# Order of TensorE's work in a two-layer gated network: output matmuls in one run of 24

## The chip, the cores and the metric

The kernel runs on one core of a Trainium2 chip. The metric is the time of one execution in device microseconds (us); of several runs the median is given. Names of engines are those of the profile: PE is TensorE (matmuls), ACT is ScalarE, DVE is VectorE, POOL is GpSimd, SP is the queue from which the transfers are issued.

## What is computed

An attention with a feature map feeds two gated networks, one after the other. Cut to what matters:

```python
def _attn_ref(q, k, v, w_phi):          # 4 batches, 8 heads, 576 tokens, 64 per head
    def phi(x):
        proj = np.einsum('bhsd,df->bhsf', x, w_phi)
        proj = proj - np.max(np.abs(proj), axis=-1, keepdims=True)
        return np.concatenate([np.exp(proj), np.exp(-proj)], axis=-1)
    q_p, k_p = (phi(q), phi(k))
    kv = np.einsum('bhsf,bhsd->bhfd', k_p, v)
    z = np.sum(k_p, axis=2)
    num = np.einsum('bhsf,bhfd->bhsd', q_p, kv)
    den = np.einsum('bhsf,bhf->bhs', q_p, z)[..., None] + 1e-06
    return (num / den).astype(np.float32)

def _moe_ref(x, w_gate, w_val, w_out):  # x: 2304 x 512; w: 512 x 1536; w_out: 1536 x 512
    g = x @ w_gate
    silu = g * (1.0 / (1.0 + np.exp(-g)))
    return (silu * (x @ w_val)) @ w_out
# _moe2_ref: the same with the gate 1 / (1 + exp(-g))
```

## The kernel before

**Two stages.** The attention takes the first 150 us or so, and the two networks the rest. While the attention runs, the weights of the first network are brought in, and its last matmuls (`ratio`) mix with the first products of the network.

**Units.** The network stage is a list of 60 units. There are four passes `hh` (two networks, each with two halves of the 1536 inner columns), five token blocks `j` in each (four of 512 tokens, called wide, and one of 256), and three slots `p` of 256 inner columns for each block. So 48 units are wide and 12 are not.

**What a wide unit does.** Its gate and value projections are not plain matrix products: both operands are cut into 2 x 2 quarters and multiplied with seven products in place of eight. The products are numbered 1 to 7. Each is 12 matmuls of 256 columns (`product`, line 1031): two halves `w` (gate and value), two depths `c`, and three matmuls for a float32 product, since every operand is held as a high and a low part (`xh`, `xl`, `w0h`, `w0l`). Products 1, 6, 7 and 4 add up in one PSUM bank `a`; 5 and 3 in a bank `b`; 2 in another bank `b`. Between them, what stands in a bank is taken out:

- `keep` (line 1051, ACT) copies a bank to SBUF tiles `c0`, `c1` after products 1, 5 and 6. After product 1 it must be done before product 6 goes on in the same bank, after 5 before 3, and after 6 before 7.
- `add` (line 1057, DVE) adds a bank to what was kept, after products 2, 3 and 7.
- `gate` (line 1069, ACT), `gated` (line 1074, DVE), and then `high` (line 583, a cast on ACT) and `rest` (line 577, a subtraction on DVE) make the high and low parts `uh0`, `ul0` (after product 2) and `uh1`, `ul1` (after product 4) of the hidden layer. Each of `c0`, `c1`, `uh0`, `ul0`, `uh1`, `ul1` is one buffer that all units share.

**Output matmuls.** The hidden layer of a unit goes through the output weights (`accumulate`, lines 1107 and 1109) while the next unit's products run: four groups "a", "b" (from `uh0`, `ul0`), "c", "d" (from `uh1`, `ul1`), six matmuls of 512 columns each in a wide unit. They add up in four PSUM banks, two tiles `c` and two `d`, over the three slots of a block, and are copied out after the third. The matmul form prints the same letters a to d for tiles; groups are in quotes here.

**What sets the order.** `ORDER` gives the order of products and groups within a unit: its first row is for the narrow units, its second for the wide ones. In a wide unit the 24 output matmuls of the unit before come in three runs: "a" and "b" (12) after products 1 and 5; "c" and half of "d" (9) after products 6, 3, 7, 2; the other half (3) after product 4. The last unit has an order of its own, `ORDER_LAST`. All instructions of the kernel, of every engine and of the transfers, are then issued in the order of a table of numbers, `TIMES`: one number for each call, sorted. The engines take their instructions in that order and wait for each other by semaphores.

Of the kernel before, what the change touches and what calls it, by code (L numbers as in the profile page):

```python
# [77 lines left out]
         (1, 5, "a", "b", 6, 3, 7, 2, "c", "d0", 4, "d1"))  # L78
# [7 lines left out]
def as_float(bits):  # L86
# [19 lines left out]
        118, 162, 249, 206, 954, 788, 1147, 1464, 2497, 1852, 2540, 3132, 3460, 3878, 3977, 4525,  # L106
        4833, 5378, 5684, 6173, 6591, 7102, 7522, 7945, 8102, 8691, 9544, 9068, 9633, 10226,
        10554, 11015, 11321, 11889, 12425, 12860,),
    "load_v": (
        292, 380, 1748, 2142, 2822, 3644, 4633, 5487, 6418, 6998, 7418, 8360, 9332, 10334, 11124,  # L110
        11785, 12191, 13289,),
    "proj": (
        601, 768, 1038, 1278, 1743, 2388, 2176, 3023, 3338, 3737, 3868, 4416, 4722, 5270, 5575,
        6065, 6482, 6993, 7413, 7837, 7925, 8582, 8933, 9436, 9524, 10117, 10416, 10907, 11212,
        11780, 12311, 12751, 13072, 13473, 14052, 14573,),
    "shift": (
        788, 1027, 1300, 1573, 2078, 2497, 2736, 3171, 3471, 3922, 4161, 4598, 4985, 5402, 5802,
        6276, 6667, 7220, 7526, 8027, 8266, 8691, 9108, 9555, 9795, 10287, 10606, 11019, 11436,
        12002, 12420, 12860, 13180, 13670, 14161, 14882,),
    "exps": (  # L120
        1038, 1189, 1283, 1433, 1748, 1856, 2329, 2450, 3053, 3239, 3732, 3882, 4664, 4814, 5487,
        5637, 6400, 6521, 7027, 7147, 7875, 8001, 8555, 8829, 9450, 9571, 10376, 10497, 11152,
        11273, 11785, 11935, 12700, 12987, 13431, 13552,),
    "k_sum": (
# [3 lines left out]
    "kv_keep": (  # L128
        2423, 2544, 3854, 4032, 5825, 5853, 7549, 7576, 9544, 9665, 11246, 11367, 13081, 13109,
        15224, 15252,),  # L130
    "turn": (
        1832, 2817, 3427, 4328, 5181, 5976, 6694, 7502, 8355, 9022, 10028, 10818, 11869, 12663,
        13561, 13963, 14484, 15219,),
    "turn_exp": (
# [4 lines left out]
    "ratio": (  # L139
# [4 lines left out]
    "ratio_out": (  # L144
# [4 lines left out]
    "ratio_store": (  # L149
# [4 lines left out]
    "den_load": (  # L154
        4790, 7042, 8889, 10598, 12468, 14658, 15446, 17825,),
    "den_inv": (
        5258, 8539, 10188, 11292, 13099, 15499, 16090, 18567,),
    "den_store": (
        5308, 8589, 10269, 11364, 13149, 15549, 16339, 18617,),
    "part_banks": (  # L160
        15433, 14716,),
    "swap": (
        15219, 17295,),
    "product": (
# [259 lines left out]
    "load_num": (  # L424
        13536, 13715, 16100, 16427, 19004, 21522, 23433, 24018, 27139, 29781,),
    "norm": (
        14400, 14460, 14761, 14821, 17132, 16837, 17192, 17620, 19596, 19562, 22152, 22186, 24214,
        24275, 24789, 24850, 27844, 27905, 30547, 30487,),
    "keep_x": (
        14532, 14897, 17235, 17692, 19641, 22318, 25949, 26375, 30041, 30467,),  # L430
# [885 lines left out]
```

## Time and profile before

| | us |
|---|---|
| median of 3 runs | 988.04 (987.86 to 988.91) |
| the profiled execution | 988.43 |
| its span, from the first to the last instruction | 986.5 |
| PE busy in it | 971.2 (98%) |
| DVE, ACT, POOL busy | 692.1 (70%), 527.6 (53%), 38.8 (4%) |
| transfers' share of 16 engines | 42.9% |
| granted TensorE clock | 1.00 of full speed |

Nearly all of the span PE is busy, in matmuls that are given to it in a fixed order. Busy time of pipelined matmuls overlaps: a matmul's row lasts 0.28 or 0.39 us, but the next one starts 0.11 or 0.23 us after it. So it is the distance between starts that tells what PE does. The rows below come from the timeline (one row for an instruction), from the chain of work that ended last (merged, with the time each piece adds), and from views that group.

### The profile page before, as it was taken

How to read it: one execution, taken by the hardware profiler on the slowest of the kernel's cores; microseconds unless marked ns; L12 is line 12 of the kernel's file. 1: busy time of each engine (PE TensorE's matmuls, PEld its weight loads, DVE VectorE, ACT ScalarE, POOL GpSimd, SP SyncE). 2: the span in 40 equal slices, each digit the busy share in tenths (PEclk: the TensorE clock that was granted, in tenths of full speed). 3: DMA queues.
4: the chain of work that ended last, by engine and by line, in shares of the span. 5: the costliest groups of instructions: out<-in, count | busy, mean ns of one | idle time of the engine just before them, and what ended most of it. 6: DMA issues, size and time to landing. Idle time of an engine off the chain costs nothing.

```text
span 986.5 us, 20911 instructions
## 1 busy us (share of the span) xinstructions
PE 971.2 (98%) x8632; PEld 883.4 (90%) x8632; DVE 692.1 (70%) x1220; ACT 527.6 (53%) x977; POOL 38.8 (4%) x40
## 2 busy tenths in 40 slices
PE   6999999999999999999999999999999999999998
PEld 6777778999999999999999999999999999999997
DVE  6989889838758795368787996576768734555343
ACT  5988878535545564354554664554546434324322
POOL 1433210000000000000000000000000000000000
PEclk9999999999999999999999999999999999999999
DMA  7566876436535532066554451546316103132011
GB/s 243 167 216 210 257 231 219 151 126 173 207 118 158 186 98 81 12 208 218 153 176 145 159 166 51 161 145 209 117 65 192 44 1 99 52 129 86 1 44 43
DMA packets 67551, 136.00 MB, mean 138 GB/s; under 512 B 9408, under 2 KB 35712, under 8 KB 67456
## 3 DMA queue, kind: packets, MB, share of 16 engines
q1 hardware_dynamic: 67456, 134.68, 42.9%
q8 instruction: 67, 1.10, 0.5%
q14 instruction: 28, 0.23, 0.1%
HBM read 94.66 MB, written 39.99 MB: 136 GB/s over the span
## 4 chain that ended last, share of the span: by engine, by line
PE 92%; DVE 6%; DMA 1%; issue 1%; ACT 0%; SPq 0%; DVEq 0%; ACTq 0%
PE a L1031 30%; PE b L1031 23%; PE c L1109 8%; PE c L1107 7%; PE d L1107 7%; PE d L1109 6%; PE d L794 4%; PE w L695 3%; PE c L731 3%; DVE sub L704 2%; DVE m L702 2%; PE w L758 1%; DMA raw<-wpk 1%; DVE w1l L577 0%; DMA x<-kT 0%
## 5 line engine op out<-in xcount | busy, mean ns | idle before, releaser
L1057 DVE TENSOR_TENSOR c<-b,c 128x512 f32<-128x512 f32 x96 | 66.0, 687 | 115.6 <-PE b L1031 108.7
L1069 ACT ACTIVATE c<-c 128x256 f32<-128x256 f32 x96 | 50.4, 526 | 145.2 <-DVE c L1057 145.2
L1051 ACT COPY c<-a 128x512 f32<-128x512 f32 x96 | 56.5, 588 | 109.1 <-PE a L1031 107.1
L577 DVE TENSOR_TENSOR ul<-c,uh 128x512 fp32r<-128x512 f32 (+1 forms) x120 | 75.8, 635 | 32.1 <-ACT uh L583 31.3
L583 ACT CAST uh<-c 128x512 fp32r<-128x512 f32 (+1 forms) x120 | 69.3, 580 | 41.7 <-DVE c L1074 32.2
L1031 PE MATMUL a<-xh,w0h 128*128 128x256 f32 x288 | 80.5, 279 | 0.0
L1031 PE MATMUL a<-xh,w1h 128*128 128x256 f32 x288 | 80.4, 279 | 0.0
L1031 PE MATMUL a<-xh,w2h 128*128 128x256 f32 x288 | 80.3, 279 | 0.0
L1031 PE MATMUL a<-xl,w0h 128*128 128x256 f32 x288 | 80.0, 278 | 0.0
L1031 PE MATMUL a<-xl,w1h 128*128 128x256 f32 x288 | 80.0, 278 | 0.0
L1031 PE MATMUL a<-xl,w2h 128*128 128x256 f32 x288 | 80.0, 278 | 0.0
L1031 PE MATMUL a<-xh,w0l 128*128 128x256 f32 x288 | 79.9, 277 | 0.0
L1031 PE MATMUL a<-xh,w1l 128*128 128x256 f32 x288 | 79.9, 277 | 0.0
L1031 PE MATMUL a<-xh,w2l 128*128 128x256 f32 x288 | 79.8, 277 | 0.0
L1074 DVE TENSOR_TENSOR c<-c 128x256 f32<-128x256 f32 (+1 forms) x96 | 53.0, 555 | 29.5 <-ACT c L1069 29.4
L1031 PE MATMUL b<-xh,w0h 128*128 128x256 f32 x224 | 62.1, 277 | 0.0
L1031 PE MATMUL b<-xh,w0l 128*128 128x256 f32 x224 | 62.0, 277 | 0.0
L1031 PE MATMUL b<-xl,w0h 128*128 128x256 f32 x224 | 62.0, 277 | 0.0
L1031 PE MATMUL b<-xh,w1l 128*128 128x256 f32 x224 | 61.9, 276 | 0.0
L1031 PE MATMUL b<-xh,w2l 128*128 128x256 f32 x224 | 61.9, 276 | 0.0
L1031 PE MATMUL b<-xh,w1h 128*128 128x256 f32 x224 | 61.9, 276 | 0.0
L1031 PE MATMUL b<-xl,w1h 128*128 128x256 f32 x224 | 61.9, 276 | 0.0
(183 smaller groups left out, 3019.7 us busy)
## 6 DMA issues: line engine op xcount, KB each, us to landing
raw<-wpk SPq DMA_DIRECT2D x72, 512.0 KB, 4.9
wf<-wcv SPq DMA_DIRECT2D x40, 256.0 KB, 2.8
a<-wf SPq DMA_DIRECT2D x20, 512.0 KB, 5.4
b<-xo SPq DMA_DIRECT2D x16, 512.0 KB, 6.9
part<-o SPq DMA_DIRECT2D x13, 512.0 KB, 6.3
o<-part SPq DMA_DIRECT2D x13, 512.0 KB, 5.3
wfo<-wcv SPq DMA_DIRECT2D x20, 256.0 KB, 5.0
v<-v SPq DMA_DIRECT2D x18, 264.0 KB, 6.6
```

The costliest lines, as they stand in the source:

```text
L577: nc.vector.tensor_tensor(out=lo, in0=src, in1=hi, op=ALU.subtract)
L583: nc.scalar.copy(hi, src)
L695: nc.tensor.matmul(r["ps"][:, i, n, c], r["x"][d, c, n * P:(n + 1) * P], w2[d], start=True, stop=True)
L731: nc.tensor.matmul(kv[qd, b][h // 2][u * 64:(u + 1) * 64, c * P:c * P + VW], e[r0:r1, h % 2, n, h // 2, s, u], r["v"][r0:r1, n, h], start= ...
L794: nc.tensor.matmul(pn[i * w:(i + 1) * w, :m], f, e[:, h, c, :m], start=(c == 0), stop=(c == 1))
L1031: nc.tensor.matmul(o, f[:, c], x[:, c], start=k == first and w == 0 and c == 0 and m == 0, stop=c == 1 and m == 2, skip_group_check=True)
L1051: nc.scalar.copy(part_of(r, d), parts(r, src))
L1057: nc.vector.tensor_tensor(out=c, in0=parts(r, "zy x"[d]), in1=c, op=ALU.add)
L1069: nc.scalar.activation(o, g, AF.Silu if hh < 2 else AF.Sigmoid)
L1074: nc.vector.tensor_tensor(out=o, in0=v, in1=places(r, j, 0, d)[1], op=ALU.mult)
L1107: nc.tensor.matmul(ps[:, :n], a[:, k], x, start=st, stop=sp)
L1109: nc.tensor.matmul(ps, x[:, k], a, start=st, stop=sp)
```

## The change

The wide row of `ORDER` is rewritten. Products 1, 5, 6, 3, 7, 2 now follow each other, all 24 output matmuls of the unit before come then in one run, and product 4 closes the unit. The order inside "a" to "d" and in a product is the same, and no matmul, copy or transfer is added or taken away. Narrow units and the last unit keep their rows. The table `TIMES` is new throughout, also for the attention; two of its rows are shown.

```diff
 ORDER = ((1, 2, "a", "b", 5, "c", "d", 4),
-         (1, 5, "a", "b", 6, 3, 7, 2, "c", "d0", 4, "d1"))
+         (1, 5, 6, 3, 7, 2, "a", "b", "c", "d", 4))
 ORDER_LAST = (1, 5, "a", 6, 3, "b", 7, 2, "c", 4, "d")
...
     "keep": (
-        15525, 15863, 16115, 16969, 17030, 17681, 18686, 18790, 19190, 20150, 20287, 20699, 21669,
...
+        15453, 15579, 15784, 16705, 16765, 17612, 18573, 18710, 18884, 20082, 20219, 20356, 21591,
```

**PE, the second unit of the fourth block in the first pass.** Each row is the first of a product's 12 matmuls, of 6 in a group, or of 3 of one bank; `a` and `b` are product banks, `c` and `d` output banks, numbers tell buffers apart. Before:

```order
L1031 MATMUL a_4146<-xh_3627,w1h0_1242 128x256
L1031 MATMUL b_4167<-xh_3627,w1h0_1242 128x256 [waits PE_49]
L1107 MATMUL c_4183<-uh0_4142,o0h0_968 128x512 [waits Activation_49]
...
L1031 MATMUL a_4146<-xh_3627,w1h0_1242 128x256 [waits Activation_49]
L1031 MATMUL b_4167<-xh_3627,w1h0_1242 128x256 [waits Activation_49]
...
L1031 MATMUL b_4241<-xh_3627,w1h0_1242 128x256 [waits PE_49]
L1107 MATMUL c_4183<-uh1_4163,o0h0_968 128x512
...
L1031 MATMUL a_4146<-xh_3627,w1h0_1242 128x256 [waits DVE_49]
L1107 MATMUL d_4197<-uh1_4163,o0h0_968 128x512
L1031 MATMUL a_4312<-xh_3627,w2h0_2645 128x256
```

and now:

```order
L1028 MATMUL a_4140<-xh_3629,w1h0_1238 128x256
L1028 MATMUL b_4158<-xh_3629,w1h0_1238 128x256 [waits PE_49]
L1028 MATMUL a_4140<-xh_3629,w1h0_1238 128x256 [waits Activation_49]
L1028 MATMUL b_4158<-xh_3629,w1h0_1238 128x256 [waits Activation_49]
...
L1028 MATMUL b_4218<-xh_3629,w1h0_1238 128x256 [waits DVE_49]
L1104 MATMUL c_4239<-uh0_4109,o0h0_945 128x512
L1104 MATMUL c_4239<-ul0_4110,o0h0_945 128x512 [waits DVE_49]
...
L1104 MATMUL c_4239<-uh1_4154,o0h0_945 128x512
...
L1028 MATMUL a_4140<-xh_3629,w1h0_1238 128x256 [waits DVE_49]
L1028 MATMUL a_4303<-xh_3629,w2h0_2665 128x256
```

The output matmuls have left the place between products 5 and 6 and the place behind product 4. Products 6 and 3, which wait for ACT's copies, stand now one product behind the product that those copies empty, as product 7 did already. In the whole program a product follows a 512-column matmul at 151 places before and at 64 now.

**ACT, the third unit of the fourth block in the third pass (the copies of the unit, `L1051` before and `L1048` now, and what stands around them).** `uh` casts make the hidden layer's high part, `xh` casts that of the next block's x, `wcv` and `raw` are steps of the weights' preparation. Before:

```order
L1069 ACTIVATE c1_8777<-a_8726 128x256 [waits PE_49]
L583 CAST uh1_8919<-c1_8777 128x512 [waits DVE_49,PE_49]
L1051 COPY c0_8930<-a_8904 128x2x256 [waits PE_49,Activation_49]
L583 CAST xh_8812<-b_8867 128x256 [waits DMAHW4_49]
L583 CAST xh_8812<-b_8867 128x512
L532 ACTIVATE wcv_8951<-raw_8747 128x512 [waits DMAHW6_49]
L1051 COPY c1_8953<-b_8922 128x2x256 [waits DVE_49,PE_49]
```

and now:

```order
L1066 ACTIVATE c1_8775<-a_8735 128x256 [waits PE_49]
L580 CAST xh_8808<-b_8852 128x256 [waits DMAHW4_49]
L580 CAST xh_8808<-b_8852 128x512
L580 CAST xh_8808<-b_8852 128x256 [waits DVE_49]
L1048 COPY c0_8935<-a_8910 128x2x256 [waits PE_49,Activation_49]
L580 CAST uh1_8944<-c1_8775 128x512 [waits DVE_49]
L580 CAST xh_8808<-t_8902 128x512
L580 CAST xh_8808<-t_8902 128x256
L1048 COPY c1_8966<-b_8926 128x2x256 [waits DVE_49,PE_49]
L1048 COPY c0_8935<-a_8910 128x2x256 [waits PE_49]
```

Here five casts of x stand between the gate and the copy after product 5, where two casts and a step of the weights stood. Over all wide units but the first, ACT has 79 such other instructions between the last gate and the copy after product 5 in 28 units before, and 41 in 19 units now; in the others the row is gate, `uh1` cast, copy, copy, copy.

## Rows read from the trace of the kernel before

**Rows 1.** Windows: length; busy us and instructions of PE, PEld, DVE, ACT, POOL; clock, DMA.

```profile
128.00:172.00 44.00, 44.00 (x597) 33.69 (x594) 39.18 (x68) 35.51 (x71) 1.53 (x2) 1.00 0.75 226
172.00:983.00 811.00, 810.55 (x5858) 759.42 (x5856) 538.77 (x1020) 388.59 (x735) 0.00 (x0) 1.00 0.37 120
```

**Rows 2.** Waits of PE from 172 to 983 us: total, times, longest.

```profile
PE c L1107 <- DVE ul L577: 0.2, 1, 0.2
```

**Rows 3.** Chain that ended last, one wide unit: start, us added, engine, matmuls.

```profile
295.93 1.39 PE a L1031 x12
...
298.00 1.39 PE a L1031 x12
299.39 1.36 PE b L1031 x12
300.75 1.37 PE c L1107 x6
302.12 1.37 PE d L1107 x6
303.50 1.39 PE a L1031 x12
304.88 1.36 PE b L1031 x12
...
311.02 1.39 PE a L1031 x12
```

**Rows 4.** PE timeline around two waits for the low part: start, us, matmul.

```profile
249.17 0.39 PE L1107 MATMUL c<-uh,o2h 128*128 128x512 f32 x1
249.50 0.50 PE L1107 MATMUL c<-ul,o2h 128*128 128x512 f32 x1
249.84 0.39 PE L1107 MATMUL c<-uh,o2l 128*128 128x512 f32 x1
...
360.96 0.39 PE L1107 MATMUL c<-uh,o2h 128*128 128x512 f32 x1
361.55 0.50 PE L1107 MATMUL c<-ul,o2h 128*128 128x512 f32 x1 [0.20 <-DVE ul L577]
361.89 0.39 PE L1107 MATMUL c<-uh,o2l 128*128 128x512 f32 x1
```

**Rows 5.** Timeline of one undisturbed wide unit, last matmuls of products 4 and 1 (PE).

```profile
739.97 0.28 PE L1031 MATMUL a<-xh,w0l 128*128 128x256 f32 x1
...
742.04 0.28 PE L1031 MATMUL a<-xh,w1l 128*128 128x256 f32 x1
```

**Rows 6.** The same on ACT: gate, cast, copies after products 1 and 5.

```profile
740.28 0.39 ACT L1069 ACTIVATE c<-a 128x256 f32<-128x256 f32 x1 [0.45 <-PE a L1031]
740.56 1.07 ACT L1142 COPY o<-d 128x512 f32<-128x512 f32 x2
741.51 0.64 ACT L583 CAST uh<-c 128x512 fp32r<-128x512 f32 x1
742.41 0.59 ACT L1051 COPY c<-a 128x512 f32<-128x512 f32 x1 [0.26 <-PE a L1031]
743.72 0.59 ACT L1051 COPY c<-b 128x512 f32<-128x512 f32 x1 [0.72 <-PE b L1031]
```

**Rows 7.** The same on DVE: `gated` and the low part.

```profile
740.70 0.43 DVE L1074 TENSOR_TENSOR c<-a,c 128x256 f32<-128x256 f32 x1
742.18 0.69 DVE L577 TENSOR_TENSOR ul<-c,uh 128x512 fp32r<-128x512 f32 x1 [1.06 <-ACT uh L583]
```

**Rows 8.** PE timeline, end of product 3 and start of 7 behind a late copy.

```profile
588.18 0.28 PE L1031 MATMUL b<-xh,w1l 128*128 128x256 f32 x1
588.33 0.39 PE L1031 MATMUL a<-xh,w1h 128*128 128x256 f32 x1
588.55 0.28 PE L1031 MATMUL a<-xl,w1h 128*128 128x256 f32 x1
```

**Rows 9.** Line 1051: ACT idle before a copy, by what ended it: us, times.

```profile
  PE a L1031: 107.1, 66
  PE b L1031: 19.3, 28
  DVE ul L577: 6.8, 9
```

**Rows 10.** ACT timeline: casts of weights, and the copy behind them.

```profile
360.55 1.05 ACT L583 CAST w2h<-a 128x1024 fp32r<-128x1024 f32 x1
361.50 0.84 ACT L583 CAST w2h<-s 128x768 fp32r<-128x768 f32 x1
362.23 0.59 ACT L1051 COPY c<-a 128x512 f32<-128x512 f32 x1
```

**Rows 11.** DVE timeline: last low part of a block's x, which PE reads from 312.94 on.

```profile
308.83 0.42 DVE L577 TENSOR_TENSOR xl<-t,xh 128x256 fp32r<-128x256 f32 x1
```

**Rows 12.** PE timeline: waits in the attention; the bracket is PE's idle time before.

```profile
43.31 1.16 PE L695 MATMUL w<-w,x 64*128 64x128 f32 x16 [1.18 <-DVE sub L704]
...
120.28 1.30 PE L794 MATMUL d<-eq,z 128*64 128x320 f32 x8 [1.16 <-ACT eq L778]
```

More of the change, by code (lines that the diff above doesn't have):

```diff
@@ L105 @@
     "load_x": (
-        118, 162, 249, 206, 954, 788, 1147, 1464, 2497, 1852, 2540, 3132, 3460, 3878, 3977, 4525,
-        4833, 5378, 5684, 6173, 6591, 7102, 7522, 7945, 8102, 8691, 9544, 9068, 9633, 10226,
-        10554, 11015, 11321, 11889, 12425, 12860,),
+        118, 162, 249, 206, 954, 788, 1147, 1464, 2497, 1852, 2540, 3132, 3447, 3878, 3934, 4605,
+        4832, 5365, 5664, 6175, 6671, 7068, 7385, 7973, 8060, 8685, 9626, 8801, 9714, 10344,
+        10432, 11010, 11315, 11863, 12274, 12753,),
@@ L109 @@
     "load_v": (
-        292, 380, 1748, 2142, 2822, 3644, 4633, 5487, 6418, 6998, 7418, 8360, 9332, 10334, 11124,
-        11785, 12191, 13289,),
+        292, 380, 1748, 2142, 2822, 3644, 4502, 5474, 6397, 7177, 7494, 8473, 8976, 10253, 11118,
+        11972, 12170, 13776,),
     "proj": (
-        601, 768, 1038, 1278, 1743, 2388, 2176, 3023, 3338, 3737, 3868, 4416, 4722, 5270, 5575,
-        6065, 6482, 6993, 7413, 7837, 7925, 8582, 8933, 9436, 9524, 10117, 10416, 10907, 11212,
-        11780, 12311, 12751, 13072, 13473, 14052, 14573,),
+        601, 768, 1038, 1278, 1743, 2388, 2176, 3023, 3338, 3737, 3825, 4497, 4723, 5257, 5556,
@@ L116 @@
+        6066, 6562, 6960, 7277, 7831, 7920, 8577, 8665, 9517, 9606, 10235, 10324, 10901, 11207,
+        11755, 12165, 12625, 13136, 13533, 13847, 14244,),
     "shift": (
-        788, 1027, 1300, 1573, 2078, 2497, 2736, 3171, 3471, 3922, 4161, 4598, 4985, 5402, 5802,
-        6276, 6667, 7220, 7526, 8027, 8266, 8691, 9108, 9555, 9795, 10287, 10606, 11019, 11436,
-        12002, 12420, 12860, 13180, 13670, 14161, 14882,),
+        788, 1027, 1300, 1573, 2078, 2497, 2736, 3171, 3471, 3922, 4161, 4605, 4958, 5451, 5732,
@@ L120 @@
+        6384, 6684, 7164, 7566, 7979, 8218, 8927, 9166, 9647, 9886, 10345, 10584, 11019, 11433,
+        11863, 12319, 12822, 13251, 13642, 13987, 14353,),
     "exps": (
-        1038, 1189, 1283, 1433, 1748, 1856, 2329, 2450, 3053, 3239, 3732, 3882, 4664, 4814, 5487,
-        5637, 6400, 6521, 7027, 7147, 7875, 8001, 8555, 8829, 9450, 9571, 10376, 10497, 11152,
-        11273, 11785, 11935, 12700, 12987, 13431, 13552,),
+        1038, 1189, 1283, 1433, 1748, 1856, 2329, 2450, 3063, 3249, 3760, 3882, 4682, 4833, 5474,
@@ L124 @@
+        5624, 6457, 6565, 7246, 7434, 7839, 7965, 8618, 8744, 9587, 9695, 10240, 10390, 11146,
+        11297, 12060, 12211, 12570, 12696, 13750, 13879,),
     "k_sum": (
[3 rows of a table removed]
[3 rows of a table added]
     "kv_keep": (
-        2423, 2544, 3854, 4032, 5825, 5853, 7549, 7576, 9544, 9665, 11246, 11367, 13081, 13109,
-        15224, 15252,),
+        2423, 2544, 3854, 3976, 5978, 6005, 7693, 7811, 9532, 9559, 11391, 11418, 13039, 13067,
+        15501, 15528,),
     "turn": (
-        1832, 2817, 3427, 4328, 5181, 5976, 6694, 7502, 8355, 9022, 10028, 10818, 11869, 12663,
@@ L133 @@
-        13561, 13963, 14484, 15219,),
+        1832, 2817, 3427, 4285, 5168, 6155, 6871, 7489, 8256, 9203, 9915, 10813, 11666, 12713,
+        13444, 14156, 14886, 14797,),
     "turn_exp": (
[4 rows of a table removed]
[4 rows of a table added]
     "ratio": (
[4 rows of a table removed]
[4 rows of a table added]
     "ratio_out": (
[4 rows of a table removed]
[4 rows of a table added]
     "ratio_store": (
[4 rows of a table removed]
[4 rows of a table added]
     "den_load": (
-        4790, 7042, 8889, 10598, 12468, 14658, 15446, 17825,),
+        4713, 6507, 8920, 10568, 12442, 13888, 15298, 18094,),
     "den_inv": (
-        5258, 8539, 10188, 11292, 13099, 15499, 16090, 18567,),
+        5351, 8544, 10159, 11706, 13061, 14893, 17222, 18497,),
@@ L426 @@
     "norm": (
-        14400, 14460, 14761, 14821, 17132, 16837, 17192, 17620, 19596, 19562, 22152, 22186, 24214,
-        24275, 24789, 24850, 27844, 27905, 30547, 30487,),
+        14286, 14226, 14832, 14592, 17101, 17161, 17689, 17628, 21909, 21875, 22637, 22604, 24372,
+        24432, 25174, 25114, 29108, 29168, 30759, 30698,),
     "keep_x": (
-        14532, 14897, 17235, 17692, 19641, 22318, 25949, 26375, 30041, 30467,),
+        14358, 14904, 17272, 17761, 21954, 22769, 25949, 26375, 30041, 30467,),
@@ L431 @@
     "load_out": (
-        15286, 34551, 36059, 37578, 55133, 56642, 58151, 75709, 77218, 78727,),
+        15211, 34478, 35907, 37416, 55007, 56516, 58025, 75664, 77173, 78682,),
 }
```

12 lines of the change are left out of this document (6 added, 6 removed), and 515 rows, old and new, of the table TIMES.

## Prediction

> **What bounds the kernel now.** I read the windows first, because they say whether anything but PE can matter. From 172 to 983 us PE is busy for 810.55 of 811 us at a granted clock of 1.00 [rows 1], and the view of waits finds one wait of PE in that whole stretch, 0.2 us for a low part [rows 2]. DVE is busy for 539 us of it and ACT for 389, so neither is a bound by its sum. The end is set by how fast PE gets through its fixed list of matmuls. Such a kernel gains only if the distance between starts of matmuls shrinks, or if a wait on PE goes. It loses whatever wait is new on PE.
>
> The chain of one wide unit shows the distances [rows 3]. Twelve product matmuls add 1.36 us where they follow other products, and 1.39 us where they follow a run of output matmuls. The unit takes 311.02 - 295.93 = 15.09 us. Its 84 product matmuls at 1.36/12 make 9.52, its 24 output matmuls at 2.74/12 (1.37 + 1.37) make 5.48, and 0.09 is left. The unit has three changes from output matmuls back to products, so one costs 0.03 us. It is the same 0.03 wherever it falls: the 1.39 at 295.93 stands behind a run of 9, at 298.00 behind 3 (the other half of "d"), at 303.50 behind 12 [rows 3]. So it belongs to the change from one kind to the other and not to the length of the run.
>
> **What the change saves on PE.** The program has 151 such places before and 64 after, 87 fewer. At 0.03 this is 2.6 us; since the rows are rounded to a hundredth, a change may cost 0.025, and then it is 2.2. I take 2.4 us.
>
> Second, two waits go. At 249.50 and 361.55 PE waits for the low part `ul0` before group "a" [rows 4]: the steps to the next two matmuls are 0.33 and 0.34 in the first case, 0.59 and 0.34 in the second, where 0.23 is the usual step. That is 0.21 and 0.47 us, in which 0.11 each time is a slow restart behind the wait. In the new order group "a" of a unit that follows a wide one stands 2.7 us or more later than before, counted from product 2, from which `uh0` and `ul0` are made; in a wide unit products 6, 3, 7 and 2 also pass ahead of it. The second wait was 0.36 long without its restart, so both are covered. This saves 0.7 us.
>
> Third, the `ratio` matmuls of the attention interrupt the first products at three places before and at one after. A restart of 0.11 is spared twice, 0.2 us.
>
> Together 3.3 us.
>
> **What the change adds on PE.** Between products 1 and 6, and 5 and 3, there were another product and the 12 matmuls of "a" and "b" (1.36 + 2.74, [rows 3]), so their copies had over 4 us. Now one product lies between: 13 steps from the last matmul of product 1 to the first of product 6, 13 x 0.113 = 1.47 us, and the same from 5 to 3. An undisturbed unit has room for this. The copy after product 1 starts 0.37 us after the product's last matmul (742.41 - 742.04) and lasts 0.59, so it ends at 0.96 [rows 5, 6]. This leaves about 0.45 us.
>
> The copy after product 5 has a second condition. It writes `c1`, which the unit before must have left, and product 4 now comes right ahead of products 1 and 5. Counted from the last matmul of product 4: the gate runs from 0.31 to 0.70 [rows 5, 6], `gated` needs 0.43 more and the cast to `uh1` 0.64 [rows 6, 7], so the cast ends at about 1.85, the copy after product 1 follows it and ends at 2.35 (due at 2.8), and the low part, 0.69 on DVE, is ready at 2.55 [rows 7]. The copy after product 5 can start at 1.36 + 1.36 + 0.32 = 3.04 at the earliest. So `c1` is free in time with half a microsecond to spare, and PE does not wait.
>
> The spare time is lost where ACT has other work in front of a copy, since it takes its instructions in order; behind such a copy are queued the next copy, the gates and the casts of the hidden layer, and PE waits for all of them. An operation of 512 columns takes about 0.5 us of ACT's row (two take 1.07 [rows 6]). Between the gate and the cast ACT idles for some 0.5 us anyway, and between the two copies for 0.7. So one or two such operations are hidden by that idle time and the 0.45. In the built order 19 wide units have other work there; in four of them it is three to six operations, and in one more it is a cast of 1024 columns, 1.05 us [rows 10], with another operation. I count those five. The price of one is bounded from below by the one late copy that the trace shows with a cover of just one product: product 7 at 588.33 lost 0.04 in its own start and 0.11 behind it [rows 8], 0.15 us. From above it is a whole cast, 1.05 - 0.45 + 0.11 = 0.7. The nearest row is between them (two or three operations too many by about 0.3); I take 0.4, so 5 x 0.4 = 2.0 us. The ends are 0.15 (a single late copy in all) and 19 x 0.7 = 13 us.
>
> On DVE and SP the same five places are crossed: `rest` for `ul1` stands among the weights' steps and the sums for x, and the loads for these are issued in the new order. Products 6, 3, 7 and 2 of a unit on a new block now read x 2.7 us earlier. The last low part of a block ended at 309.24 where its block began at 312.94 [rows 11], 3.7 us ahead, and no other wait for x is on PE [rows 2]. I cost it at nothing; without that cover it would be up to a microsecond, four times at most.
>
> The attention's order is new too. Its PE waits after the first 16 us are a few of at most 1.2 us, the two largest 1.18 and 1.16 [rows 12]. The work is the same, so I put the difference at 0 with a bound of 1 us either way.
>
> **Sum.** 988.43 (the profiled execution; its span is 986.5) - 3.3 + 2.0 = 987.1 us. The profiled run lies 0.4 above the median of 988.04, so as a median the forecast is 986.7 us.
>
> **The rivals.**
>
> *The copies are nearly always in time.* For it: with one product as cover, product 7 was late visibly once in 48 units [rows 8], and the new order puts less foreign work in front of the copies, 41 operations against 79. Against it: a copy after product 5 was held by `ul1` nine times [rows 9], at a time when it had 3.4 us from product 4, and now it has 2.7. The loss falls to 0.3, and the time is 988.04 - 3.3 + 0.3 = 985.0 us.
>
> *The copies are as late as they were.* This is the way to slower. Only 94 of the 144 copies found ACT waiting for PE [rows 9]; 50 came late, which cost nothing under the old cover. At 362.23 a copy started behind two weight casts [rows 10], 2.7 us after the last matmul of its product (13 steps before the group at 360.96 [rows 4]). The change is slower once the copies cost 3.3 + 2.0 (0.2% of the time, about what a measurement here can tell from no change) = 5.3 us, which is 0.11 per wide unit, one restart in each. If ACT and DVE are late in all 19 units with foreign work by 0.35 plus a restart, the loss is 19 x 0.46 = 8.7, and the time 988.04 - 3.3 + 8.7 = 993.4 us.
>
> *The changes cost nothing that merging can return.* The 0.03 could be paid for something else that stays, for instance for the 24 output matmuls as such, settled in the products behind them. Then 2.4 falls out: 986.7 + 2.4 = 989.1 us. Against it: the step is the same behind runs of 12, 9 and 3. The Trainium skill ("TensorE: Matmul & The Clock Gate", section "Wait — 56ns, not 53.3ns?") points this way: it gives a matmul's distance to the next as its columns over the clock plus a fixed 2.5 ns, whatever ran before, by which an order could return nothing. Here the step at 512 columns is 228 ns where the page has 215.7, and the steps do depend on what ran before [rows 3].
>
> **How the numbers follow.** Forecast 0.54, with a range of its own from 985.7 to 988.0; copies in time 0.24; copies late 0.10; nothing returned 0.12. Faster by over 0.2% means below 986.06: the second case and a tenth of the first, 0.30. Slower by over 0.2%, above 990.02: the third, 0.10. Within: 0.60. The range must hold 0.8; it takes in the forecast with the microsecond of the attention, the copies in time and the case in which nothing is returned, and leaves out the late copies and little else: 985.0 to 989.3.
>
> **What would show it.** In the chain of the changed kernel a wide unit should show one run of products with 1.39 for 12, behind product 4's place, and 1.36 elsewhere, and a period of 15.03 us in place of 15.09; if the periods are still 15.09, the third rival holds. The view of waits should name ACT's copies as what product 6 or 3 waited for, at about five places and 1.5 us in all; much more is the second rival, none the first. No wait for `ul0` should be left near 250 and 361. The forecast is wrong altogether if the first product starts more than a microsecond earlier or later by the work done so far, or if PE waits for x or weights at the start of a block.

## The result and the profile after

The changed kernel is slower: median 997.85 us (995.06 to 998.78) against 988.47, ratio 1.0082 with a 95% interval of 1.0071 to 1.0094. A second set gave 996.66 against 989.28, ratio 1.0072 (1.0053 to 1.0092). The forecast was 986.7, and its range ended at 989.3.

First the page's row for PE, and the two windows of [rows 1] with the second carried on to 990 us (length; busy us and instructions of PE, PEld, DVE, ACT, POOL; clock, DMA). The profiled execution took 995.06 us, its span is 993.2:

```profile
PE 975.2 (98%) x8632; PEld 885.6 (89%) x8632; DVE 690.6 (70%) x1220; ACT 528.9 (53%) x977; POOL 39.6 (4%) x40
...
128.00:172.00 44.00, 41.62 (x558) 32.06 (x556) 37.47 (x65) 30.27 (x57) 1.30 (x1) 1.00 0.62 175
172.00:990.00 818.00, 814.76 (x5854) 761.47 (x5852) 537.92 (x1022) 391.72 (x741) 0.00 (x0) 1.00 0.37 121
```

PE is still busy nearly all of the time, at full clock. In the first window it now idles for 2.4 us, in the second for 3.2 of 818 where it was 0.45 of 811. But over the whole span its busy time has grown too, from 971.2 to 975.2 us for the same matmuls. So 4.0 of the 6.7 us by which the span grew don't show as idle time. The view of waits for the second window (total, times, longest), which answers [rows 2]:

```profile
PE a L1028 <- ACT c L1048: 2.2, 3, 1.2
PE c L1104 <- ACT o L1139: 0.2, 1, 0.2
PE a L1028 <- DVE c L1054: 0.2, 1, 0.2
```

The copies are named, as in the second rival. Next the chain that ended last (start, us added, engine, matmuls), which answers [rows 3], in a unit at 616 us and in one at 690 us:

```profile
616.99 1.36 PE b L1028 x12
...
623.79 1.37 PE c L1106 x6
...
629.29 1.73 PE a L1028 x15
...
690.64 1.41 PE b L1028 x12
...
696.29 1.41 PE b L1028 x12
697.71 2.77 PE c L1106 x12
700.47 2.83 PE a L1028 x24
```

The first unit is as forecast. The second has no wait in it, and yet all its products take 1.41 us for 12 matmuls, where 1.36 is usual. So there are stretches in which each 256-column matmul takes 0.118 us and not 0.113. They are most of what the idle time leaves out.

From the starts of all 5,545 product and output matmuls between the fourth unit's first product and the last unit's first, I summed what each step (start to next start) takes beyond 113.4 ns for 256 columns and 228.4 ns for 512:

| us | before | after | after, second trace |
|---|---|---|---|
| length of the stretch | 764.69 | 769.38 | 768.88 |
| waits, with the slow step behind them | 0.83 (6 steps) | 4.00 (21) | 5.14 (25) |
| stretches at 118 ns | 0.83 (181) | 4.26 (967) | 2.79 (633) |
| the slow steps behind a run of output matmuls | 4.02 (792) | 1.66 (332) | 1.81 (355) |
| output matmuls | 0.80 | 1.23 | 0.94 |
| start of the stretch | 197.01 | 199.07 | 200.06 |

The four terms and the rest (-0.2 each) add up to the difference of the lengths, 4.69 us. The gain is there, 2.36 us in the fourth row; waits cost 3.2 us, slow stretches 3.4, and some 2 us are lost ahead of the stretch.

### The profile page after: what moved, and what is told of

Its sections match the earlier page's. It is cut to its first block, busy times and chain, and to the rows that moved or that the text cites. A ratio compares the mean times of both kernels' runs of the same rounds, so it can differ in the third digit from the quotient of the medians.

```text
span 993.2 us, 20912 instructions
## 1 busy us (share of the span) xinstructions
PE 975.2 (98%) x8632; PEld 885.6 (89%) x8632; DVE 690.6 (70%) x1220; ACT 528.9 (53%) x977; POOL 39.6 (4%) x40
## 4 chain that ended last, share of the span: by engine, by line
PE 86%; DVE 6%; DMA 3%; ACT 2%; issue 1%; SPq 1%; DVEq 0%; ACTq 0%
PE a L1028 27%; PE b L1028 21%; PE c L1106 8%; PE d L1106 6%; PE d L1104 6%; PE c L1104 6%; PE d L791 4%; PE w L692 3%; PE c L728 3%; DVE sub L701 1%; DMA rb<-rden 1%; DVE m L699 1%; PE w L755 1%; DMA b<-xo 1%; DMA raw<-wpk 1%
## 5 line engine op out<-in xcount | busy, mean ns | idle before, releaser
L1066 ACT ACTIVATE c<-c 128x256 f32<-128x256 f32 (+1 forms) x96 | 50.1, 524 | 117.4 <-DVE c L1054 117.3
L1066 ACT ACTIVATE c<-a 128x256 f32<-128x256 f32 x60 | 23.0, 383 | 134.1 <-PE a L1028 134.1
L1071 DVE TENSOR_TENSOR c<-a,c 128x256 f32<-128x256 f32 x60 | 25.4, 423 | 82.4 <-ACT c L1066 82.0
L1048 ACT COPY c<-a 128x512 f32<-128x512 f32 x96 | 56.4, 587 | 30.9 <-PE a L1028 29.4
L1071 DVE TENSOR_TENSOR c<-c 128x256 f32<-128x256 f32 (+1 forms) x96 | 52.8, 554 | 24.2 <-ACT c L1066 23.9
L1028 PE MATMUL b<-xh,w2h 128*128 128x256 f32 x224 | 62.4, 279 | 0.0
```

The lines of the kernel that those rows point to most:

```text
L1028: nc.tensor.matmul(o, f[:, c], x[:, c], start=k == first and w == 0 and c == 0 and m == 0, stop=c == 1 and m == 2, skip_group_check=True)
L1048: nc.scalar.copy(part_of(r, d), parts(r, src))
L1066: nc.scalar.activation(o, g, AF.Silu if hh < 2 else AF.Sigmoid)
L1071: nc.vector.tensor_tensor(out=o, in0=v, in1=places(r, j, 0, d)[1], op=ALU.mult)
```

## The experiments

The theory at this point: ACT's copies come late because they lie behind other work in its row. The rivals: the new order of the attention; and that a long run of output matmuls itself brings the 118 ns. All kernels in one table; waits, stretches at 118 ns and steps behind runs are sums as above, from one trace each, and ratios are against runs of the kernel before on the same chip (medians 989.0 to 989.7):

| kernel | median us (range) | ratio, 95% | waits | 118 ns | behind runs |
|---|---|---|---|---|---|
| after_again | 996.7 (994.4-997.9) | 1.0072 (53-92) | 5.14 | 2.79 | 1.81 |
| attn_new | 992.4 (991.5-995.6) | 1.0032 (21-44) | 1.07 | 1.07 | 3.89 |
| attn_old | 995.8 (991.0-999.1) | 1.0061 (40-81) | 4.26 | 5.53 | 1.65 |
| half_d1 | 995.3 (994.1-997.8) | 1.0060 (46-74) | 5.76 | 5.37 | 2.23 |
| copies_first | 999.8 (996.6-1002.0) | 1.0104 (83-124) | 8.67 | 1.06 | 1.97 |
| half_d1_copies | 996.1 (993.4-998.1) | 1.0065 (48-82) | 8.07 | 0.72 | 2.95 |
| p2_attn_old | 990.6 (989.0-994.5) | 1.0018 (6-29) | 3.59 | 1.26 | 1.87 |
| copy_thrice | 1001.2 (1001.1-1002.9) | 1.0125 (109-140) | 13.35 | 0.84 | 4.16 |
| after_c1_two | 993.8 (992.0-996.2) | 1.0040 (25-54) | 3.47 | 4.46 | 1.67 |
| one_run_c1 | 991.6 (989.6-994.4) | 1.0023 (10-35) | 2.89 | 6.28 | 1.48 |
| p2_c1 | 990.0 (987.7-999.5) | 1.0006 (-15 to 27) | 3.36 | 1.10 | 1.87 |
| half_d1_c1 | 992.4 (990.2-995.8) | 1.0035 (20-49) | 4.13 | 0.94 | 2.83 |
| copy_steps | 1003.5 (1003.2-1003.7) | 1.0135 (115-154) | 12.63 | 2.20 | 3.75 |
| p2_last | 989.6 (988.6-998.4) | 1.0003 (-14 to 19) | 4.66 | 1.09 | 1.82 |
| before_c1 | 991.6 (989.8-993.5) | 1.0017 (6-28) | 2.58 | 1.17 | 3.93 |
| after_split | 995.1 (993.2-996.2) | 1.0056 (41-72) | 3.88 | 1.52 | 3.06 |
| one_run_split | 991.4 (990.5-993.1) | 1.0024 (14-34) | 3.19 | 1.53 | 3.00 |
| p2_split | 988.7 (986.2-990.1) | 0.9988 (-22 to -2) | 0.61 | 0.31 | 2.92 |

(Intervals in the last digits: 53-92 is 1.0053 to 1.0092.)

The traced run of a kernel is not its median run. It was the fastest of p2_attn_old and p2_split and the slowest of half_d1, after_c1_two and one_run_c1, so the last three columns explain that run and not the median beside it. Of the 4.66 us of p2_last, 1.6 are steps at half the granted clock and no waits.

### The attention, and what merging is worth alone

`after_again` is the changed kernel. 

> The changed kernel once more, unaltered. Every theory expects 995 to 998 us, as in its four runs on record (995.06 to 998.78). It is run for its trace: three of those four runs were about 3 us longer than the profiled one and had a granted clock of 0.998 and not 1.000. If a stretch at the lower clock level is the cause of those 3 us, the profile of a run of 997 or 998 us shows one stretch with steps of twice the length, and an idle TensorE ahead of it; if the 3 us are more waits for copies of the products' banks, the clock is 1.000 and the table of waits has more of them.

The run of 994.4 us lies below the range, the others in it. The traced run took 995.51 us and had a clock of 1.000; of the two long ones, one (997.81) had 0.998 and the other (997.94) 1.000. So a lower clock is not what makes the long runs long, at least not in that one, and as no long run is traced, what does stays open.

`attn_new` (on the kernel before) and `attn_old` (on the changed one) swap the table's numbers for the attention and the first four units, and with them the order of these units:

```diff
+ORDER_FIRST = (1, 5, 6, 3, 7, 2, "a", "b", "c", "d", 4)
...
+ORDER_FIRST = (1, 5, "a", "b", 6, 3, 7, 2, "c", "d0", 4, "d1")
```

> The new order of the attention part and of the first block's first four units, on the kernel before for everything behind them (its order of a wide unit, three runs of output matmuls). Theory of the late copies: the loss of the changed kernel sits in the wide units, so this kernel loses only what the first product is later, 0.6 us, and what the first units wait: 988.9 to 990.5. Rival, the new attention order: most of the 6.6 to 9 us are lost through what the new order hands to the units behind it, or through a stretch of lower clock there: 994 to 997.

> The other way round: the attention part and the first four units in the old order, everything behind them as in the changed kernel (one run of 24 in a wide unit). Theory of the late copies: most of the loss stays, 993 to 996. Rival, the new attention order: the loss is gone and the 2 us of fewer changes show, 986 to 988.

Both theories hold a part: attn_new came out between its two ranges, attn_old in the first. The new order of the attention and the first four units costs 3.1 us alone, the order of the wide units behind them 6.5 us alone, and both together 7.4 to 9.4. The place in the attention is its end. PE timelines of the changed kernel and of after_again (the bracket is PE's idle time before):

```profile
145.95 3.16 PE L728 MATMUL c<-v,ek 128*64 128x66 f32 x96
150.41 0.39 PE L1028 MATMUL a<-xh,w0h 128*128 128x256 f32 x1 [1.30 <-ACT eq L775]
```

```profile
151.86 0.38 PE L1028 MATMUL a<-xh,w0h 128*128 128x256 f32 x1 [1.69 <-ACT eq L775]
```

The first product waits for ACT's `eq` in all six traces of the new order and starts at 150.4 to 153.3 us, 151.9 in the mean; in the 14 traces of the old one it starts at 149.2 to 151.1 us, 150.2 in the mean. By the fourth unit's first product the means are 200.5 and 197.6.

`half_d1` takes the kernel before and merges its runs of 9 and 3 alone:

```diff
-         (1, 5, "a", "b", 6, 3, 7, 2, "c", "d0", 4, "d1"))
+         (1, 5, "a", "b", 6, 3, 7, 2, "c", "d0", "d1", 4))
```

> The kernel before with one thing altered: in a wide unit the second half of the last group of output matmuls stands ahead of product 4, not behind it, so that the output matmuls come in two runs of 12, not in three of 12, 9 and 3. The covers of the copies stay as in the kernel before. It takes away 46 changes from output matmuls to products. If a change costs what the rows of before show (0.025 us), this kernel takes 46 x 0.025 = 1.1 us less than the kernel before: about 987.3 against 988.4. If changes cost nothing that merging gives back, it takes 988.4. If the halves of the gate and value work behind product 4, now 0.7 us later, hold back the next unit's copies, it is slower, at up to 0.1 us a wide unit, 993.

Undisturbed units fell from 15.09 to 15.07, so a change costs about 0.025 us, as forecast. (The sum behind runs fell by 1.8 us and not by 1.1, since in a slow stretch these steps are counted there; in half_d1_copies, which has little of it, it fell by 1.1.) Still the kernel is 6 us slower: 13 steps at waits, and from a wait at 768.65 us to the end every one of 1,000 and more product steps at 118 ns.

### Why the copies are late

`copies_first` moves 64 rows of the table, and 14 that depend on them: casts and conversions close ahead of a copy come behind it. Of its `high` row:

```diff
-        78864, 79952, 80409, 81460, 81917,
+        78864, 79952, 80501, 81460, 81917,
```

> The changed kernel with 64 rows of the order table altered: where ScalarE had a cast (`high`) or a weight conversion (`mag`, `tail`) standing so close ahead of a copy `keep` that it would not be over when the copy's product is, that cast now stands right behind the copy. Nothing else moves. Theory of the late copies: between 190 and 970 us TensorE waits for 4.4 us in the changed kernel and for 1.2 us in the kernel before, because copies stand in ScalarE's row behind casts; with the copies first those waits fall below 2 us, and with them the stretches in which 256-column steps take 118 ns and not 113 ns, which begin only at such waits (4.3 us against 0.8 us): 995 falls to 989 to 992, what is left over 988.4 being lost ahead of 200 us. Rival, the waits come from VectorE, late with the adds and the gated products, and ScalarE's row only shows it: the waits stay, 994 to 997.

This missed: the waits about doubled, though the stretches at 118 ns nearly went. The view of the copies' line says until what ACT sat idle before a copy (us, times), from 190 us on, in the changed kernel and then in copies_first:

```profile
  PE a L1028: 24.3, 38
  PE b L1028: 19.2, 28
  DVE ul L574: 6.2, 8
```

```profile
  PE a L1028: 33.5, 54
  DVE ul L574: 27.6, 31
  PE b L1028: 8.9, 13
```

In [rows 9], 66 copies of bank `a` found ACT waiting for the product (64 of them from 190 us on); now 38 do, and the others are late. With the copies first, `uh1` is cast later, so `ul1` is later, and the copy after product 5, which overwrites `c1`, waits for it 31 times: PE lost 6.5 us at product 3, in 20 places. Not all of its loss is of this kind. Its span is 4.8 us longer than the changed kernel's, and 2.8 of them lie ahead of the fourth unit: there PE idled for 1.96 us up to 152.41, and from 153.6 to 155.1 us the granted clock was 0.50. Casts and copies can't both come first; the chain gate, `gated`, `uh1`, `ul1`, copy has become too long for the new distance. In the changed kernel PE lost 0.8 us at product 3 (6 places), 2.2 at product 6 (4) and 0.6 at product 7 (2).

What makes that chain late is partly DVE. The chain that ended last, before the wait at 319.60 us:

```profile
302.10 7.11 DMA rb<-rden
...
311.13 0.94 DVE xl L574 x2
312.06 0.33 DVE c L1071
...
317.13 0.34 DVE wcv L537
317.47 0.05 DVE ul L574
...
317.99 0.43 DVE c L1071
...
318.96 0.59 ACT c L1048
...
319.60 1.64 PE a L1028 x12
```

A load that landed late pushes the sums and splits of x together on DVE; `gated` (L1071) stands behind them, the cast to `uh1` waits for `gated`, and the copy stands behind the cast. The old order had 4.2 us of cover here, the new one 1.47.

`half_d1_copies` gives half_d1 the same moves. 

> half_d1 (two runs of 12 in a wide unit) with the copies first in ScalarE's row, as in copies_first. half_d1 came out at 995.3 although its undisturbed units were 0.025 us shorter: nine waits of TensorE and a stretch of 118 ns steps from 768 us to the end. If the copies behind casts are the cause of all of that, this kernel shows what two runs of 12 are worth alone: 988.4 - 1.1 = 987.3, range 986.5 to 989. If the waits have another source, 992 to 996.

 It came out just above the second range. The waits grew, in part for `ul1` and `uh1` themselves, which the output matmuls read (2.6 us of idle time). Product 4 behind the half group made the same chain late for another reader.

`after_c1_two` takes the chain's condition away, on the changed kernel:

```diff
-            r["c", f] = pools["u"].tile([P, 2, 2, NQ], F32, tag=f"c{f}", name=f"c{f}")
+            r["c", f] = pools["u"].tile([P, 2, 2, NQ], F32, tag=f"c{f}", name=f"c{f}",
+                                          bufs=1 + f)
```

and the cast to `uh1` stands behind copy 5.

> The changed kernel with two things altered: the tile `c1`, in which copy 5 puts its part and from which the unit before casts `uh1` and takes `ul1`, has two buffers, so copy 5 no longer waits for `ul1`; and the cast to `uh1` stands behind copy 5 in ScalarE's row, not ahead of copy 1. Nothing in the attention part or in the order of TensorE moves. Theory of the chain behind product 4 (gate, gated, uh1, ul1 and only then copy 5, which the changed order asks for 1.4 us after product 5 and the old one 4.2 us): the waits of TensorE for copies between 190 and 970 us (4.4 us in the changed kernel) fall below 2 us, the stretches at 118 ns with them, and the time is 990 to 994; the 3 us of the attention order stay. Rival, background casts and late x blocks make the copies late: waits stay above 3.5 us, 995 to 998.

The time fell by 3 us, into the range of the theory, and no wait at product 3 is left in the trace. But the reason given was half wrong: waits fell only to 3.5 us (now at product 7, 1.9, and 6, 1.3), and the traced run has 4.5 us at 118 ns.

`p2_attn_old` goes the other way and gives cover back: old attention order, copies first, and

```diff
-         (1, 5, 6, 3, 7, 2, "a", "b", "c", "d", 4))
+         (1, 5, 2, 6, 3, 7, "a", "b", "c", "d", 4))
```

> Old attention order; one run of 24 in a wide unit, but with product 2 between products 5 and 6 (order 1, 5, 2, 6, 3, 7, a to d, 4), which gives the copies of products 1 and 5 two products (2.7 us) of cover and not one, and copies first in ScalarE's row. If late copies are all that stood against the change: 988.4 - 2.3 (93 changes fewer) = 986.1, range 985.5 to 988. If the single run itself brings the 118 ns steps, or product 6's copy, still under one product, is late: 990 to 995.

The time lies in the second range. With one more product ahead of 6 and 3, 5 of attn_old's 6.5 us are back; since the same moves made copies_first slower, I put that down to the cover, which no run here tries alone. `one_run_c1`, `p2_c1` and `half_d1_c1` join the second buffer with the old attention order. 

> The old attention order; from the fifth unit on the wide unit of the changed kernel (products 1, 5, 6, 3, 7, 2, one run of 24, 4), with two buffers for `c1`, the cast to `uh1` behind copy 5, and weight casts and conversions that stood close ahead of a copy put behind it. If the chain behind product 4 and the casts ahead of copies are all that the merged run pays: 988.4 - 2.4 (changes) = 986, range 985.5 to 988. If one product is too short a cover even so: 989 to 994.

> As one_run_c1, with product 2 between products 5 and 6, so that the copies of products 1 and 5 have two products of cover and only product 6's has one. p2_attn_old, the same order without the second buffer, came out at 990.6 with 4 us of waits. Theory of the chain behind product 4: 985.5 to 987.5. If what is left there came from x blocks that land late (the longest wait, 1.5 us at 586.6 us, stood behind a cast that waited for a load): 988 to 990.5.

> half_d1 (two runs of 12, old attention order) with the second buffer of `c1`, the cast to `uh1` behind copy 5 and the background casts behind the copies. half_d1 alone: 995.3; with the copies ahead of the casts alone: 996.1, with waits of 2.5 us for `ul1` itself, which the output matmuls read, and 2.1 us for product 6's copy. Theory of the chain: moving product 4 behind the second half of the last output group left `ul1` late for the third group of the next unit too (1.3 us late at 250 and 364 us), which a second buffer doesn't cure: 991 to 995. If the copies alone mattered: 987 to 989.

Only the third did what the theory of the chain says. one_run_c1 has the fewest waits of the kernels that have the changed kernel's wide unit, and the most time at 118 ns. p2_c1 is level with the kernel before, with two waits left: 1.8 us for a copy behind casts that waited for a load, 1.6 us for copies of output sums. `p2_last` moves both, `before_c1` gives p2_c1's other edits to the kernel before. 

> p2_c1 with its two longest waits taken away: at 587.6 us (1.77 us) the copy of product 6 stood behind casts that waited for an x block's load, they now stand behind the copy; at 256.6 us (1.48 us) output matmuls waited for the copies of the sums of the block before, which now stand ahead of casts. If waits and the pace after them were all that the merged run paid: 990.0 - 3.2 = 986.8, range 985.5 to 988, below the kernel before. If other waits take their place: 988.5 to 991.

> The kernel before with what p2_c1 has beside the merged run: two buffers for `c1`, the cast to `uh1` behind copy 5, weight casts and conversions behind the copies. It tells how much of a gain or loss of p2_c1 and p2_last is theirs and not the merged run's. The kernel before waits 1.2 us between 190 and 970 us, so at most 1 us is to be had: 987.5 to 989.5. If the moved casts make new waits, as in copies_first: 990 to 993.

p2_last stayed where p2_c1 was: the wait for the load went, and the one for the output sums grew to 2.9 us, so that move was a mistake. before_c1 is slower than the kernel before, so the other edits bring nothing by themselves. p2_last, which has them too, is 2.0 us faster on the same chip: the merged run with product 2 moved seems to return something, though p2_last also has two moves of its own.

### Where the 118 ns come from

`copy_thrice` and `copy_steps` make waits in the kernel before, in 15 units; of copy_steps:

```diff
         nc.scalar.copy(part_of(r, d), parts(r, src))
+        if k == 6 and r.get("n") is not None:
+            nc.scalar.copy(part_of(r, d), parts(r, src))
+            n = NQ - 4 * r["n"]
+            nc.scalar.copy(part_of(r, d)[:, :, :n], parts(r, src)[:, :, :n])
```

> The kernel before, with the copy of product 6 made three times over in 15 wide units (the blocks from 610 to 655, 683 to 771 and 771 to 861 us), so that its third copy ends after product 3 and TensorE waits for it, once a unit, for some tenths of a us. Theory of the pace: after a wait TensorE starts again in one of two paces, 113 or 118 ns for a 256-column step, and keeps it through runs of output matmuls until it next waits. Then some of these 15 units have all of their product steps at 118 ns and are 0.36 us longer than the wait alone makes them, although their output matmuls come in three runs. Rival, the 118 ns stretches belong to the single long run of output matmuls: no unit here has more than its 15 steps after the runs at 118 ns.

> As copy_thrice (the kernel before, product 6's copy three times over in 15 wide units), but the third copy takes 512 columns in the first of the 15 units, 504 in the second and 8 fewer in each that follows, 400 in the last, so that the wait of TensorE ends some ns earlier from unit to unit. In copy_thrice all waits were alike (0.72 us, the second step after the release 108 or 109 ns over) and all 15 units went on at 113 ns. Theory that the moment of the release sets the pace: the second step is 113 ns over in some of the 15 units, those units go on at 118 ns in all 84 product steps, 0.36 us a unit, through all three runs of output matmuls, and the others at 113 ns. Rival, the pace belongs to the long run of output matmuls: no unit goes on at 118 ns.

In copy_thrice the 15 units went on at 113 ns, as the rival expected. In copy_steps, whose waits are 4 to 9 ns shorter from one unit to the next (0.72 to 0.62 us, and one of 1.01), ten went on at 118 ns and five at 113. The PE timeline of copy_steps at a wait of each sort, and the chain behind the first:

```profile
709.61 0.39 PE L1032 MATMUL a<-xh,w1h 128*128 128x256 f32 x1 [0.53 <-ACT c L1056]
709.84 0.28 PE L1032 MATMUL a<-xl,w1h 128*128 128x256 f32 x1
...
636.96 0.38 PE L1032 MATMUL a<-xh,w1h 128*128 128x256 f32 x1 [0.55 <-ACT c L1056]
637.18 0.28 PE L1032 MATMUL a<-xl,w1h 128*128 128x256 f32 x1
```

```profile
711.29 1.42 PE b L1032 x12
712.71 1.39 PE c L1114 x6
714.10 0.69 PE d L1114 x3
714.79 1.42 PE a L1032 x12
716.20 0.70 PE d L1114 x3
716.90 1.38 PE a L1032 x12
```

The released matmul (the first behind the wait) takes 0.23 us to the next in the slow case, 0.22 in the other; to the nanosecond it is 225 or 226 in the ten slow units and 220 or 221 in the five others. Over all 20 traces, in the stretch of the first table, of the product steps that were 112 to 114 ns over the usual one, 19 of 19 went on at 118 ns; of those with 107 to 111 ns, 12 of 103. So the longer released step is a mark of the slow pace; that it is the cause is not shown. What copy_steps shows is that the moment of the release decides, in the order of the kernel before too. It is not a matter of a longer or shorter wait: behind PE idle times of 554 ns and of 541 to 514 the pace was slow, behind 550, 509 and 503 it was usual.

The pace of 1.42 goes on through the run of 9 and product 4, and is 1.38, the usual value behind a change, after the run of 3. It is so in nine of the ten slow units; in the tenth a run of 3 stands in the place of the run of 9 and ends it.

A wait is not the only way into the slow pace. In the kernel before it begins in the narrow units, where output matmuls have 256 columns and PE waits for nothing (its chain):

```profile
257.09 0.68 PE d L1107 x6
257.77 1.42 PE a L1031 x12
...
259.90 0.70 PE d L1107 x6
260.60 1.37 PE a L1031 x12
```

Behind twelve such matmuls the pace turned from one to the other at 165 of 169 places in the 20 traces. Nearly all of the 0.83 us at 118 ns in the kernel before come from there, and a part of every other kernel's.

copy_steps points to a second thing that the change removed: the old order's run of 3. `after_split` and `one_run_split` put it back into the merged orders:

```diff
-         (1, 5, 6, 3, 7, 2, "a", "b", "c", "d", 4))
+         (1, 5, 6, 3, 7, 2, "a", "b", "c", "d0", 4, "d1"))
```

> The changed kernel with the last of its 24 matmuls of a wide unit's run split off: a run of 21 ahead of product 4 and a run of 3 behind it, where the kernel before has its run of 3. Nothing else of the change is undone. In copy_steps ten units went on at 118 ns after a wait, through the run of 9, and all ten were back at 113 ns behind the run of 3. Theory that the run of 3 ends the slow pace: no stretch at 118 ns outlives its unit; between 190 and 970 us the steps at 118 ns outside the five behind each run cost under 1.5 us, not the 2.8 to 4.8 us of the changed kernel's traces; the waits stay near 4 us, and 46 changes more cost 1.1 us: 994 to 997. Rival, only a wait ends it: stretches of several units remain, 2.5 us or more, 996 to 998.

> one_run_c1 with the same split (runs of 21 and 3). one_run_c1 lost 6.6 us to stretches at 118 ns in its trace with only 2.9 us of waits, and its runs lay between 989.6 and 994.4. If the run of 3 ends the slow pace: under 1.5 us of it, 1.1 us more for the changes, 988 to 990 and the runs closer together. If only a wait ends it: 990 to 995 as before, 1 us higher.

The chain of one_run_c1 at 399 us, and that of one_run_split from 543 us on:

```profile
399.17 1.41 PE b L1029 x12
400.59 1.39 PE c L1106 x6
401.98 1.37 PE d L1106 x6
...
406.10 2.83 PE a L1029 x24
```

```profile
543.58 1.54 PE b L1032 x12
...
545.82 1.40 PE c L1109 x6
547.22 1.40 PE d L1109 x6
...
550.72 1.38 PE a L1032 x12
552.10 0.69 PE d L1109 x3
552.79 1.39 PE a L1032 x12
```

In one_run_c1 one slow stretch begins at 317 us and outlives nine runs of 24. In the kernels with a run of 3 none outlives its unit, wherever that run has 512 columns, and the sum at 118 ns is 1.5 us in both. But it was not the run of 3 that did it in the merged orders. In one_run_split's chain product 4 at 550.72, ahead of that run, is back at 1.38 already, where copy_steps has 1.42. In the traces of the two kernels nine of the ten slow stretches that met a run of 21 ended behind it, and only the tenth behind the run of 3.

Such a run tells by its own steps whether the slow pace will pass it. In the rows six output matmuls take 1.37 us behind the first six in one_run_c1, and 1.40 all through in one_run_split. Over all traces, in runs of 24 and 21 that a slow stretch met, the output steps took 229.6 or 229.7 ns in the mean in 40, and the slow pace came out of all of them; they took 233.3 or 233.4 in 30, and it ended in all. In the changed kernel's trace the stretches that began behind the waits at 218 and 440 us, with released steps 109 and 108 ns over the usual, are of the second sort, and those from 541 and 650 us, both 113 over, of the first. So the slow pace comes in two sorts. The nine stretches above were of the sort that a run of 24 ends as well, so the two kernels put the run of 3 to the test only once.

The median of one_run_split is no better and lies in the second range, since 46 changes are back (1.5 us behind runs), but its runs lie within 2.6 us where they lay within 4.8.

`p2_split` has the run of 3, the longer cover, the second buffer and the old attention order, and the casts that waited for a load behind the copy. 

> p2_c1 with the split (products 1, 5, 2, 6, 3, 7, a run of 21, product 4, a run of 3) and the casts that waited for an x block's load at 587 us behind the copy. Against the kernel before it has 46 changes fewer (1.1 us), longer covers for two copies and the same run of 3 in each unit. If waits and pace are all that decides: 987.5 to 989, level with the kernel before or a little below. If moving the sums' copies by the split makes new waits: 989.5 to 992.

It is the one kernel with a median below the kernel before: 988.71 against 989.04, ratio 0.9988 (0.9978 to 0.9998). One in 18 kernels with an interval that ends so near 1 is weak evidence of a gain; level is the safer reading. Its trace, of the fastest run (986.17), has 0.6 us of waits and 0.3 us at 118 ns.

## Why the prediction was wrong

- **What bounds the kernel: right.** The span still is what PE's list takes, and the loss is in PE's steps and waits.
- **The changes, 2.4 us: right,** 2.36 measured; undisturbed wide units went from 15.09 to 15.04 us. So the third rival fell. The Trainium skill ("TensorE: Matmul & The Clock Gate", section "Wait — 56ns, not 53.3ns?") has one fixed addition for each matmul; the steps here have two paces, 113.4 and 117.7 ns, and more behind a change.
- **The waits for `ul0`, 0.7 us: right.** After the change the steps of group "a" of [rows 4] are regular (the changed kernel's PE timeline):

```profile
251.45 0.39 PE L1104 MATMUL c<-uh,o2h 128*128 128x512 f32 x1
251.68 0.39 PE L1104 MATMUL c<-ul,o2h 128*128 128x512 f32 x1
251.91 0.39 PE L1104 MATMUL c<-uh,o2l 128*128 128x512 f32 x1
```

- **The late copies, 2.0 us: mis-sized.** They cost 3.6 and 4.2 us in the two traces, at 12 and 13 places. The step that failed is the count of places: I counted units with foreign work on ACT's row in the built order, and took the chain behind product 4 as free "with half a microsecond to spare", from one undisturbed unit [rows 5 to 7]. Nine copies that had waited for `ul` [rows 9] already said that the chain was the tight place, and I read them as an argument against the first rival only. Four of the five units that I counted are among the 12 places, near 541, 650, 721 and 899 us. But the largest wait, 1.5 us at 319.60, is in none: no foreign work stands on ACT's row there, and DVE, late by a late load, was costed at nothing.
- **The price of a wait: a term that was missing.** I gave a wait its length and a restart of 0.11 us. It can also leave PE at 118 ns, 0.36 us for each wide unit that follows, until a later wait or run of output matmuls ends it. Beyond what the kernel before has of it, that was 3.4 us in one trace of the changed kernel and 2.0 in the other. The second rival's point of decision, 5.3 us of waits, was never reached by the waits alone.
- **The attention, 0 with a bound of 1: wrong.** It cost 2 to 3 us at the end of the attention and in the first units. The first product started 0.6 and 2.0 us later than before in the two traces. The prediction named a shift of over a microsecond there among what would make it wrong, and gave it no case.
- **The rivals.** The second named the mechanism and the sign, at 993.4 us and a chance of 0.10. With the measured terms the sum is 988.4 - 3.3 + 3.6 (copies) + 2.1 (start of the stretch) + 3.4 (pace) = 994.2 for the first trace and 988.4 - 3.3 + 4.2 + 3.1 + 2.0 = 994.4 for the second, against the profiled 995.06 and 995.51. The rest, about 1 us, is in the main other waits and slower output matmuls. What the runs of 997.8 to 998.8 have beyond that is not traced and stays open.

## What to carry to other kernels

A gap in a list of matmuls that looks like a cost may be doing two jobs: it covers the work of other engines, and, as the run of 3 did in copy_steps, it can bring TensorE back to its pace. Before merging, list for each buffer what must be over in the shortened distance, from the late units of the trace and not from a quiet one. And when an engine has never waited, don't price its first wait by its length: try what the steps do behind it.

## What the runs showed of the hardware

- 256-column matmuls go at 113.4 or 117.7 ns a step, 512-column ones at 228 to 229 or, between slow products, up to 5 ns more. The moment of a release decides which, and so do runs of output matmuls of 256 columns without any wait; the pace can last hundreds of matmuls. What in the engine does it is not shown.
- A run of 3 output matmuls of 512 columns ended the slow pace at 12 of 12 places, and runs of 6 and 9 kept it at 28 of 29. Runs of 12, 21 and 24 kept it or ended it: with steps of 229.6 to 230.5 ns in the mean they kept it (76 of 76), with 233.3 they ended it (40 of 40). Why is open.
- The granted clock fell to 0.50 (1.2 GHz of 2.4) in stretches of a few us behind idle times of PE. In p2_last PE idled for 2.63 us ahead of 260.21; windows from 259.7 and 262 us (length; busy us and instructions as above; clock):

```profile
259.70:261.60 1.90, 1.39 (x9) 1.39 (x10) 0.09 (x1) 1.90 (x5) 0.00 (x0) 0.85 0.07 28
262.00:264.00 2.00, 2.00 (x12) 2.00 (x11) 2.00 (x5) 2.00 (x6) 0.00 (x0) 0.50 0.69 207
```
